# Attention and two MoE layers on one core: another hand-planned order of the steps up to the last block

## The chip, the cores and the metric

One core of a Trainium2 chip runs the whole program in one launch. The metric is the device time in microseconds. Three runs of the kernel before took 759.48, 760.04 and 760.96 us; the profile is of one further execution.

## What is computed

```
scores = (q @ k.T) / 8 + alibi, only 0 <= i - j < 128      # 4 batches, 8 heads, 576 rows, head size 64
x  = softmax(scores) @ v                                   # as [2304, 512]
x  = (relu(x @ w_in) ** 2) @ w_out                         # w_in 512 x 2048, w_out 2048 x 512
on = x @ w_skip > 0                                        # second MoE, 8 experts of 512 x 1024 x 512
e  = argmax(x @ w_gate); g = softmax(x @ w_gate)[e]
out = x;  out[on] += g * (relu(x @ w1[e]) @ w2[e])
```

## The kernel before

The 2304 rows are 18 tiles of 128; two tiles are a block, so there are nine blocks. Every fp32 factor of a large product is split into a high part and the rest (fp32r), and a product takes three matmuls: high x high, high x rest, rest x high.

The program up to the last block is a list of **steps**. A string of 1647 steps (line 879) is read from left to right by `piece` (line 1000), and each step issues its instructions under `manual_schedule` (line 1026), so the list sets the order in each of the five queues (TensorE, VectorE, ScalarE, Pool, SP). Between queues only the data's semaphores hold: an instruction starts when it is the first of its queue and its inputs and buffers are ready. A step's letter says what it is, the numbers which, and a last letter v, a or p puts it on VectorE, ScalarE or Pool where there is a choice:

- Attention of tile t: `l` loads q and k, or v (SP, L379, L382); `H` takes the high part of q and k (kh, L74), `L` the rest (kl, L392); `S` is the scores (TensorE, L408); `D` adds the bias and takes the row's extreme (VectorE from PSUM, L437); `E` the exponentials (ScalarE, L448); `M`, `N` guard and invert the sum (L458, L462); `O` normalises (L475 on ScalarE, L477 on VectorE, two instructions); `T` transposes (TensorE, L484), `U` copies that out (pts, L74); `V` multiplies by v (TensorE, L509); `Y` and `Z` write the two parts of the block's x (L74, L531).
- Weights of the first MoE, 32 chunks that come as 64-bit words: `w` loads (SP, L849), `j a b c d` turn them into floats in place (L94 or L96, then VectorE L100, L103, L108, L113), `e` and `f` write the two parts (L74, L125; `f` on Pool unless marked).
- First MoE of block n, pair fp of hidden chunks: `A` twelve products into ph (TensorE, L564), `r s g i` relu, square, high part gh, rest gl (L574, L580 or L582, L74, L592), `B` twelve products into acc (TensorE, L616).
- Routing of block n: `P Q` copy acc out, `p` (TensorE, L668), `q` copies lgs (ScalarE, L675), `m` (TensorE, L680), `o C F G J K k` choose experts and ranks, `W` writes the lists (Pool, L795); `t` transposes x2T (TensorE, L699), `x` copies it to xt (ScalarE, L706) and issues its two transfers, to x2d and to out (L709, L710). There is one xt buffer.

Behind the list stand the last block's first MoE, in which the first experts' weights are already loaded and split (from line 1048), and the second MoE expert by expert (from line 1129). Neither is touched.

All 32 weight chunks are converted while blocks 0 and 1 are multiplied, so for the first 133 us VectorE has both this and the softmax to do; after that TensorE's products set the pace.

Of the kernel before, what the change touches and what calls it, by code (L numbers as in the profile page):

```python
# [19 lines left out]
def attn_moe_kernel(  # L20
# [262 lines left out]
    with ExitStack() as mctx, ExitStack() as actx:  # L283
# [574 lines left out]
        def split(c):  # L858
# [27 lines left out]
            Z0 M1.2 w7 j7 w8 a7 U1.1 N1.2 H3.0 d5 b7 c4 w9 E2.1 c7 O1.2a N2.0 U1.0 d4 M2.1 j9 j6
            l1.1 V1.0 O1.3 a9 T1.3 N2.1 a6 O2.0a U1.3 T1.2 f1 U1.2 O2.1a b9 e4v w12 w10 L2.1
            S2.1 b6 H3.1 V1.1 e5v c6 c9 f0 d2 Y1a T2.0 U2.0 T2.1 j8 Z1 d9 A0.0.0 A0.0.1 w11 j11
            U2.1 D2.3 E2.3 a11 a8 D2.2 l2.1 V2.0 M2.3 e2 f3 b8 E2.2 N2.3 O2.3a d7 r0.0 M2.2 w13
            c8 j10 L3.0 S3.0 N2.2 O2.2a d6 d8 a10 T2.3 U2.3 s0.0a g0.0 e8v b10 D3.0 e9 b11 c10  # L890
            E3.0 f4 A0.1.0 T2.2 U2.2 D3.1 E3.1 j12v c11 a12 L3.1 j13 e7v M3.0 b12 M3.1 f2 N3.0
            f5 e6 c12 A0.1.1 a13 O3.0a f8 j16 A0.2.0 N3.1 d11 V2.1 i0.0p B0.0.0 S3.1 b13 r0.1
            O3.1a d10 T3.0 U3.0 D3.2 B0.0.1 Y2a E3.2 a16 T3.1 c13 s0.1a Z2 M3.2 U3.1 d13 g0.1v
            e13 e11 N3.2 O3.2a d12 i0.1 f9 A0.2.1 e12v r0.2 D3.3 E3.3 s0.2a f12v b16 M3.3 l3.1
            V3.0 f6 B0.1.0 w17 w15 T3.2 U3.2 j17v N3.3 A0.3.0 e10v a17 b17 c16 O3.3a g0.2 i0.2
            c17 f7 f13 A0.3.1 j14 a14 T3.3 b14 U3.3 f11 B0.2.1 j15 a15 b15 w18 c15 c14 r0.3 V3.1
            B0.1.1 Y3a Z3 d14 f10 B0.2.0 A1.0.0 A1.0.1 s0.3a d15 d17 g0.3 i0.3 e15 f15v j18 e14
            d16 f14v e17 A1.1.0 e16 A1.1.1 r1.0 s1.0a f16v a18 w19 B0.3.1 g1.0 i1.0 b18 j19 r1.1
            s1.1a c18 d18 e18 a19 b19 c19 d19 f17 B0.3.0 e19v f19v w20 g1.1 w21 j20v a20 j21 a21
            b20 b21 c20 c21 d20 e20 A1.2.0 f18 A1.2.1 A1.3.0 i1.1p d21 w22 w23 j22v A1.3.1  # L900
            B1.0.0 e21 B1.1.0 f20v a22 b22 B1.0.1 j23 r1.2 c22 f21v a23 B1.1.1 s1.2a g1.2 i1.2
            B1.2.1 r1.3 A1.4.0 s1.3a A1.4.1 b23 c23 A1.5.0 d22 g1.3v B1.2.0 l4.1 e22 d23 f22v
            w25 j25 e23v a25 b25 c25 d25 w24 j24 a24 i1.3 B1.3.1 e25v A1.5.1 B1.3.0 b24 c24 d24
# [344 lines left out]
```

## Time and profile before

| | |
|---|---|
| median of three runs | 760.04 us (759.48 to 760.96) |
| the profiled execution | 760.54 us, of which the instructions span 758.6 us |
| TensorE busy | 704.0 us, 93% of the span |
| VectorE, ScalarE, Pool busy | 447.4, 370.0, 178.9 us |
| granted TensorE clock, mean | 0.990 |
| the list of steps | ends at about 541 us; the rest takes 217.6 us |

The profile names an instruction by engine, line and tiles (`gl<-r,gh`: gl is written, r and gh are read) and gives its start and length in us. PE is TensorE, DVE VectorE, ACT ScalarE, POOL GpSimd. In brackets stands how long the engine had been idle before the instruction and what released it. An instruction that is blocked once it has been issued shows no idle time: it is only longer.

### The profile page before, as it was taken

How to read it: one execution, taken by the hardware profiler on the slowest of the kernel's cores; microseconds unless marked ns; L12 is line 12 of the kernel's file. 1: busy time of each engine (PE TensorE's matmuls, PEld its weight loads, DVE VectorE, ACT ScalarE, POOL GpSimd, SP SyncE). 2: the span in 40 equal slices, each digit the busy share in tenths (PEclk: the TensorE clock that was granted, in tenths of full speed). 3: DMA queues.
4: the chain of work that ended last, by engine and by line, in shares of the span. 5: the costliest groups of instructions: out<-in, count | busy, mean ns of one | idle time of the engine just before them, and what ended most of it. 6: DMA issues, size and time to landing. Idle time of an engine off the chain costs nothing. (4 is left out here: it accounts for less than half of the span.)

```text
span 758.6 us, 14480 instructions
## 1 busy us (share of the span) xinstructions
PE 704.0 (93%) x5620; PEld 639.6 (84%) x5620; DVE 447.4 (59%) x1140; ACT 370.0 (49%) x803; POOL 178.9 (24%) x166
## 2 busy tenths in 40 slices
PE   4588999998999999999999999999999789999994
PEld 3376999887999999999998999998999567777773
DVE  8999999664563544544354456332547627538871
ACT  6887555453453455343523434432346427437751
POOL 5364210222103402112022323211310511211220
PEclk9999999999999999999999999999999989999998
DMA  9513344014010130201010110024336377719840
GB/s 353 214 46 122 100 165 140 29 43 153 29 42 16 57 111 2 70 1 44 29 42 16 56 43 16 1 71 143 108 108 213 113 279 253 274 34 315 317 155 5
DMA packets 27682, 82.11 MB, mean 108 GB/s; under 512 B 4188, under 2 KB 4444, under 8 KB 27584
## 3 DMA queue, kind: packets, MB, share of 16 engines
...
HBM read 69.31 MB, written 12.49 MB: 108 GB/s over the span
## 5 line engine op out<-in xcount | busy, mean ns | idle before, releaser
L616 PE MATMUL acc<-gh,w2h_out 128*128 128x256 f32 x576 | 97.8, 292 | 0.9 <-ACT gh L74 0.8
L564 PE MATMUL ph<-xh,w1h_in 128*128 128x256 f32 x576 | 95.0, 287 | 0.6 <-DVE w1h_in L74 0.6
L616 PE MATMUL acc<-gl,w2h_out 128*128 128x256 f32 x576 | 92.8, 283 | 0.9 <-DVE gl L592 0.8
L564 PE MATMUL ph<-xh,w1l_in 128*128 128x256 f32 x576 | 92.5, 282 | 0.3 <-DVE w1l_in L125 0.3
L616 PE MATMUL acc<-gh,w2l_out 128*128 128x256 f32 x576 | 92.2, 282 | 0.0
L564 PE MATMUL ph<-xl,w1h_in 128*128 128x256 f32 x576 | 91.9, 282 | 0.0
L592 POOL TENSOR_TENSOR gl<-r,gh 128x512 fp32r<-128x512 f32 x33 | 44.1, 1336 | 189.4 <-ACT gh L74 110.0
L448 ACT ACTIVATE pr<-pr,stat 128x256 f32<-128x256 f32 (+1 forms) x144 | 70.1, 489 | 38.0 <-DVE stat L437 37.8
L574 ACT ACTIVATE r<-ph 128x512 f32<-128x512 f32 x72 | 42.7, 593 | 91.2 <-PE ph L564 57.8
L616 PEld LDWEIGHTS acc<-gh,w2h_out 128*128 128x128 f32 x576 | 78.6, 190 | 1.8 <-ACT gh L74 1.3
L616 PEld LDWEIGHTS acc<-gl,w2h_out 128*128 128x128 f32 x576 | 78.8, 189 | 1.5 <-DVE gl L592 1.5
L564 PEld LDWEIGHTS ph<-xh,w1l_in 128*128 128x128 f32 x576 | 78.6, 188 | 1.1 <-DVE w1l_in L125 0.5
L564 PEld LDWEIGHTS ph<-xh,w1h_in 128*128 128x128 f32 x576 | 78.4, 189 | 1.2 <-ACT sz L94 0.8
L616 PEld LDWEIGHTS acc<-gh,w2l_out 128*128 128x128 f32 x576 | 78.7, 189 | 0.0
L564 PEld LDWEIGHTS ph<-xl,w1h_in 128*128 128x128 f32 x576 | 78.5, 188 | 0.0
L484 PE MATMUL pt<-ident,pr 128*128 128x128 f32 x272 | 47.0, 296 | 8.0 <-ACT pts L74 5.6
L509 PE MATMUL pv<-pts,vt 128*64 128x128 f32 x544 | 40.1, 289 | 8.6 <-ACT pts L74 7.4
L158 DVE TENSOR_TENSOR w1l_e<-raw_e,w1h_e 128x1024 fp32r<-128x1024 f32 x31 | 36.7, 1224 | 16.2 <-ACT w1h_e L157 16.2
L475 ACT ACTIVATE pr<-pr,stat 128x256 f32<-128x256 f32 (+1 forms) x80 | 34.4, 482 | 23.6 <-DVE stat L462 23.3
L484 PEld LDWEIGHTS pt<-ident,pr 128*128 128x128 f32 x272 | 32.0, 148 | 16.0 <-ACT pts L74 6.9
L582 POOL TENSOR_TENSOR r<-r 128x512 f32<-128x512 f32 x17 | 18.0, 1056 | 114.2 <-ACT r L574 114.2
L509 PEld LDWEIGHTS pv<-pts,vt 128*64 128x64 f32 x544 | 30.0, 141 | 15.4 <-ACT pts L74 8.6
...
## 6 DMA issues: line engine op xcount, KB each, us to landing
...
big_w1l<-in_w_mlp_dram SPq DMA_DIRECT2D x4, 512.0 KB, 10.3
```

The lines of the kernel that those rows point to most:

```text
L158: eng.tensor_tensor(lo, val, hi.bitcast(F32), op=ALU.subtract)
L448: nc.scalar.activation(pr[:, j, cols], pr[:, j, cols], AF.Exp, bias=st[:, 0, h : h + 1], scale=-1.0, accum_out=st[:, 1, h : h + 1],)
L475: nc.scalar.activation(p, p, AF.Copy, scale=r[:, c])
L484: nc.tensor.transpose(pt[:, j, o : o + P], pr[:, j, o : o + P], ident)
L509: nc.tensor.matmul(to, a, b_, start=(kk == kts[0]), stop=(kk == t), skip_group_check=True,)
L564: nc.tensor.matmul(ph[:, j, :], a[:, kc, fs], b_[:, kc, :], start=(j == 0 and kc == 0 and a is wh and b_ is xh), stop=(kc == KC - 1 and a ...
L574: nc.scalar.activation(r, phs.pop((n, fp)).rearrange("p a b -> p (a b)"), AF.Relu)
L582: eng.tensor_tensor(r, r, r, op=ALU.mult)
L592: eng.tensor_tensor(gl.rearrange("p a b -> p (a b)"), r, gh.rearrange("p a b -> p (a b)").bitcast(F32), op=ALU.subtract,)
L616: nc.tensor.matmul(acc[dc // 2][:, dc % 2, :], a[:, f0 + j, dsl], b_[:, j, :], start=(fp == 0 and j == 0 and dc % 2 == 0 and b_ is gh and ...
```

## The change

The string of steps is another one: the same 1647 steps, in a different order, planned with a margin of time kept around every Pool instruction. Nothing else differs. Some steps change their engine: `L` 18 times on Pool for 21, `f` 19 for 17, `s` 19 for 17, `i` 32 for 33; `U` 20 times on VectorE for 30; `O` 34 on VectorE for 32.

```diff
@@ -877,113 +877,113 @@
         order = """
-            l0.0 H0.1 H0.0 L0.0v w0 j0 l1.0 S0.0 H1.0 a0 b0 D0.0 w1 E0.0 D0.1 c0 w2 l2.0 L1.0v
...
+            l0.0 H0.0 L0.0v S0.0 H0.1 w1 j1 a1 b1 D0.0 D0.1 l1.0 H1.0 E0.0 M0.0 L0.1 L1.0v w0
...
         """
```

What moves is seen in the queues. The first place is ScalarE at the routing of block 0 (`x0.1` is the second COPY of xt before, `q0` the COPY of lgs). Before:

```order
L706 COPY xt_1_2232<-xp_1_2215 128x512
L709 DMA x2d<-xt_1_2232 128x512
L710 DMA out_dram<-xt_1_2232 128x512
L574 ACTIVATE r_1_2250<-ph_1_2199 128x512
L706 COPY xt_1_2268<-xp_1_2258 128x512
L709 DMA x2d<-xt_1_2268 128x512
L710 DMA out_dram<-xt_1_2268 128x512
L675 COPY lgs_2297<-lgp_2253 128x256
L448 ACTIVATE pr_1_2187,stat_2181<-pr_1_2187,stat_2181 128x256 x2
```

and now:

```order
L706 COPY xt_1_2262<-xp_1_2256 128x512
L709 DMA x2d<-xt_1_2262 128x512
L710 DMA out_dram<-xt_1_2262 128x512
L475 ACTIVATE pr_0_2147<-pr_0_2147,stat_2146 128x256 x2
L574 ACTIVATE r_1_2296<-ph_1_2204 128x512
L675 COPY lgs_2320<-lgp_2251 128x256
L448 ACTIVATE pr_2_2317,stat_2146<-pr_2_2317,stat_2146 128x256 x2
```

Before, lgs stood right behind two copies of xt that follow each other with one relu between; now the earlier copy of xt is further ahead, and a normalisation and a relu stand between xt and lgs. The second place is ScalarE at the end of the list, the routing of block 6 (`x6.1`, `x5.0`, `q6`). Before:

```order
L706 COPY xt_1_6518<-xp_1_6449 128x512
L709 DMA x2d<-xt_1_6518 128x512
L710 DMA out_dram<-xt_1_6518 128x512
L574 ACTIVATE r_6_6535<-ph_6_6415 128x512
L580 ACTIVATE r_6_6535<-r_6_6535 128x512
L706 COPY xt_0_6556<-xp_0_6546 128x512
L709 DMA x2d<-xt_0_6556 128x512
L710 DMA out_dram<-xt_0_6556 128x512
L675 COPY lgs_6563<-lgp_6548 128x256
```

and now:

```order
L706 COPY xt_1_6459<-xp_1_6425 128x512
L709 DMA x2d<-xt_1_6459 128x512
L710 DMA out_dram<-xt_1_6459 128x512
L726 ACTIVATE ex_6467<-dl_6464 128x16
L74 CAST gh_5_6495<-r_5_6423 128x512
L574 ACTIVATE r_6_6552<-ph_6_6440 128x512
L74 CAST gh_6_6555<-r_6_6552 128x512
L675 COPY lgs_6575<-lgp_6547 128x256
L726 ACTIVATE ex_6609<-dl_6606 128x16
L574 ACTIVATE r_7_6611<-ph_7_6481 128x512
L706 COPY xt_0_6613<-xp_0_6523 128x512
L709 DMA x2d<-xt_0_6613 128x512
```

The copy of lgs moved ahead of `x5.0`, and two relus, two high parts and two exponentials stand between the two copies of xt. The third place is Pool from the chunks of the second half of the weights to the last one (`w1l_in` and `w2l_out` are steps `f`, gl is `i`). Before:

```order
L125 TENSOR_TENSOR w1l_in_1007<-raw_1_846,w1h_in_1006 128x4x128
L125 TENSOR_TENSOR w2l_out_1009<-raw_2_925,w2h_out_1008 128x512
L592 TENSOR_TENSOR gl_1_1091<-r_1_1063,gh_1_1090 128x512
L125 TENSOR_TENSOR w2l_out_1009<-raw_3_1150,w2h_out_1008 128x512
L125 TENSOR_TENSOR w1l_in_1007<-raw_1_1308,w1h_in_1006 128x4x128
L592 TENSOR_TENSOR gl_5_1397<-r_5_1393,gh_5_1396 128x512
```

and now:

```order
L592 TENSOR_TENSOR gl_3_943<-r_3_925,gh_3_942 128x512
L125 TENSOR_TENSOR w1l_in_988<-raw_0_412,w1h_in_987 128x4x128
L125 TENSOR_TENSOR w1l_in_988<-raw_1_375,w1h_in_987 128x4x128
L592 TENSOR_TENSOR gl_0_1074<-r_0_1041,gh_0_1073 128x512
L592 TENSOR_TENSOR gl_1_1093<-r_1_1089,gh_1_1092 128x512
L125 TENSOR_TENSOR w2l_out_990<-raw_2_1222,w2h_out_989 128x512
L125 TENSOR_TENSOR w2l_out_990<-raw_2_1381,w2h_out_989 128x512
L125 TENSOR_TENSOR w1l_in_988<-raw_0_1436,w1h_in_987 128x4x128
L592 TENSOR_TENSOR gl_6_1499<-r_6_1470,gh_6_1498 128x512
```

In this stretch Pool has nine instructions for six, three of them two rests gl (`i`) and one rest of a weight more; with `f10`, and now also `f11`, which stand between Z3 and the rows shown, it is 11 for 7.

## Rows read from the trace of the kernel before

**Rows 1.** Busy time by stretch: each engine, (xN) instructions, granted PE clock, DMA share, GB/s.

```profile
0.00:80.00 80.00, 55.22 (x440) 46.10 (x441) 73.50 (x198) 61.20 (x157) 38.02 (x47) 1.00 0.46 174
80.00:135.00 55.00, 52.97 (x439) 52.18 (x438) 53.46 (x92) 29.71 (x50) 11.36 (x7) 1.00 0.44 141
135.00:515.00 380.00, 376.88 (x3455) 356.14 (x3454) 187.35 (x642) 163.46 (x433) 80.53 (x68) 1.00 0.13 43
```

**Rows 2.** Waits of PE up to 80 us: us in all, times, longest; first and last of nine.

```profile
PE pv L509 <- ACT pts L74: 7.0, 2, 5.9
...
PE acc L616 <- DVE gl L592: 0.6, 1, 0.6
```

**Rows 3.** The same view from 80 to 541 us; first and last of seven.

```profile
PE lgp L680 <- ACT lgs L675: 4.0, 2, 2.2
...
PE acc L616 <- DVE gl L592: 0.3, 1, 0.3
```

**Rows 4.** Timeline of PE, 0 to 120 us: start, us, engine, line, operation.

```profile
84.75 0.64 PE L616 MATMUL acc<-gh,w2h_out 128*128 128x256 f32 x4
85.23 0.64 PE L616 MATMUL acc<-gh,w2l_out 128*128 128x256 f32 x4
```

**Rows 5.** Timeline of all engines, 25.3 to 34.2 us.

```profile
25.63 1.37 POOL L125 TENSOR_TENSOR w1l_in<-big_w1h,w1h_in 128x512 fp32r<-128x512 f32 x1 [8.74 <-issue]
...
27.23 0.42 DVE L437 CUSTOM_DVE_ANT_0 pr<-sc,bias 128x256 f32<-128x256 f32 x1
...
28.18 1.74 POOL L125 TENSOR_TENSOR w1l_in<-big_w1h,w1h_in 128x512 fp32r<-128x512 f32 x1
...
28.70 1.51 DVE L74 CAST w2h_out<-big_w1h 128x512 fp32r<-128x512 f32 x1
...
33.53 0.41 DVE L103 TENSOR_SCALAR sz<-sz 128x512 int32<-128x512 int32 x1
33.86 0.68 DVE L108 SCALAR_TENSOR_TENSOR big_w1l<-big_w1l,sz 128x512 int32<-128x512 int32 x1
```

**Rows 6.** The same view, 13.9 to 15.6 us.

```profile
14.01 1.53 DVE L103 TENSOR_SCALAR sz<-sz 128x512 int32<-128x512 int32 x1
```

**Rows 7.** The same view, 132.8 to 135 us.

```profile
132.71 0.69 DVE L125 TENSOR_TENSOR w2l_out<-raw,w2h_out 128x512 fp32r<-128x512 f32 x1
...
133.32 1.52 DVE L74 CAST kh<-raw 128x512 fp32r<-128x512 f32 x1
```

**Rows 8.** The same view, 76 to 82 us.

```profile
77.86 0.68 DVE L531 TENSOR_TENSOR xl<-pv,xh 128x512 fp32r<-128x512 f32 x1
```

**Rows 9.** The same view, 173 to 186.5 us.

```profile
176.66 0.41 DVE L74 CAST kh<-raw 128x512 fp32r<-128x512 f32 x1
...
177.23 0.59 ACT L706 COPY xt<-xp 128x512 f32<-128x512 f32 x1
...
183.96 0.58 ACT L706 COPY xt<-xp 128x512 f32<-128x512 f32 x1 [4.59 <-DMA out_dram<-xt]
...
185.86 0.61 PE L680 MATMUL lgp<-sel,lgs 128*128 128x9 f32 x4 [2.18 <-ACT lgs L675]
```

**Rows 10.** The same view, 508 to 545 us.

```profile
530.12 0.58 ACT L706 COPY xt<-xp 128x512 f32<-128x512 f32 x1 [4.15 <-DMA out_dram<-xt]
...
532.02 0.61 PE L680 MATMUL lgp<-sel,lgs 128*128 128x9 f32 x4 [1.83 <-ACT lgs L675]
```

**Rows 11.** Groups by line and form, 0 to 560 us: xcount, busy us, mean ns, idle.

```profile
L448 ACT ACTIVATE pr<-pr,stat 128x256 f32<-128x256 f32 x128 | 63.9, 501 | 37.0 <-DVE stat L437 37.0
...
L592 POOL TENSOR_TENSOR gl<-r,gh 128x512 fp32r<-128x512 f32 x33 | 44.1, 1336 | 189.4 <-ACT gh L74 110.0 <-DVE gh L74 53.6 <-PE sc L416 12.4
L574 ACT ACTIVATE r<-ph 128x512 f32<-128x512 f32 x68 | 40.3, 593 | 84.7 <-PE ph L564 51.3 <-DVE gl L592 14.6 <-POOL gl L592 14.0
...
L477 DVE TENSOR_SCALAR pr<-pr,stat 128x256 f32<-128x256 f32 x62 | 25.8, 458 | 0.7
...
L592 DVE TENSOR_TENSOR gl<-r,gh 128x512 fp32r<-128x512 f32 x35 | 24.1, 688 | 14.9 <-ACT gh L74 13.9 <-issue 0.7
```

More of the change, by code (lines that the diff above doesn't have):

```diff
@@ L886, in attn_moe_kernel @@
[L886 to L903, printed above, removed]
@@ L958, in attn_moe_kernel @@
-            i5.4 A5.6.0 D13.1 E13.1 M13.1 A5.5.1 S13.1 H14.1v L14.1 r5.5 N13.1 O13.1 V12.1 T13.0
-            Y12 Z12 U13.0 D13.2 E13.2 s5.5p g5.5 i5.5 B5.4.0 T13.1 l13.1 D13.3 B5.4.1 A5.6.1
-            M13.2 N13.2 O13.2 E13.3 M13.3 U13.1 B5.5.1 V13.0 r5.6 s5.6a T13.2 U13.2v A5.7.0
-            A5.7.1 N13.3 O13.3a T13.3 U13.3v S14.0 g5.6v D14.0 E14.0 D14.1 V13.1 i5.6p r5.7 Y13
-            t4.0.0 B5.6.0 Z13 B5.5.0 A6.0.0 A6.0.1 s5.7a H15.0v L15.0 E14.1 M14.1 t4.0.3 S14.1
-            p4 t4.0.1 M14.0 l16.0 N14.0 t4.0.2 g5.7v i5.7p x4.0 B5.6.1 r6.0 l14.1 s6.0p g6.0
@@ new lines, in attn_moe_kernel @@
+            B0.0.0 O3.1a s0.1a f3 g0.1 i0.1 w19 f9 A0.2.1 Y2a B0.0.1 T3.1 Z2 D3.3 j13 a13 E3.2
+            M3.2 b13 E3.3 U3.1 M3.3 N3.2 O3.2a w15 N3.3 c13 d13 b16 e13v f12 j17v a17 f6 B0.1.0
+            O3.3a l3.1 A0.3.0 e10v V3.0 T3.2 U3.2 c16 r0.2 s0.2a g0.2 j14 f7 B0.1.1 d11 i0.2
+            e11v a14 b14 b17 c17 T3.3 U3.3 c14 f13 A0.3.1 r0.3 s0.3a V3.1 Y3a Z3 j15 j18 g0.3
+            d14 e14 d17 a15 d16 b15 f10 f14v a18 c15 j19v d15 a19 e15v B0.2.0 f11 B0.2.1 f15v
+            b19 e17 c19 A1.0.0 b18 c18 i0.3p d18 d19 e18v f18v A1.0.1 e16 f16 A1.1.0 f17 r1.0
@@ new lines, in attn_moe_kernel @@
+            s1.0a w20 j20v e19v B0.3.0 A1.1.1 g1.0 i1.0p B0.3.1 r1.1 s1.1a g1.1 a20 B1.0.0
+            B1.0.1 A1.2.0 b20 c20 A1.2.1 f19v w21 j21 a21 b21 w23 c21 A1.3.0 A1.3.1 d20 i1.1p
+            B1.1.0 r1.2 s1.2a g1.2v d21 B1.1.1 e20 f20v i1.2 e21 f21v w22 j22 a22 j23 a23 b22
+            r1.3 b23 c23 s1.3a g1.3 A1.4.0 A1.4.1 w25 i1.3 j25 B1.2.1 r1.4 w24 c22 d22 a25 d23
+            B1.2.0 b25 e22 j24 a24 e23 b24 f23v A1.5.0 B1.3.0 c24 s1.4a g1.4 c25 d25 e25v A1.5.1
+            d24 i1.4 B1.4.0 B1.3.1 f25v w26 e24 f24v A1.6.0 A1.6.1 r1.5 f22 j26v a26 b26 c26
@@ new lines, in attn_moe_kernel @@
+            E6.0 D6.1 t1.1.0 t1.1.2 t1.1.3 A2.0.0 t1.1.1 x1.1 A2.0.1 r2.0 P0 l8.0 Q0 s2.0 g2.0v
+            A2.1.0 l7.0 J1 H7.0v A2.1.1 S6.1 E6.1 p0 t0.1.0 t0.1.3 t0.1.1 M6.0 t0.1.2 x0.1 i2.0
+            B2.0.0 B2.0.1 N6.0 O6.0a r2.1 T6.0 A2.2.0 D6.2 q0 A2.2.1 E6.2 M6.2 m0 s2.1p g2.1v
+            i2.1 B2.1.0 B2.1.1 A2.4.0 A2.4.1 r2.2 s2.2p A2.3.0 M6.1 N6.1 O6.1a g2.2v N6.2 i2.2p
+            B2.2.1 o0 B2.2.0 C0 F0 G0 l6.1 U6.0v T6.1 r2.4 K0 s2.4 g2.4 O6.2 U6.1 k0 i2.4 D6.3
+            E6.3 A2.3.1 B2.4.0 W1 L7.0 t0.0.0 t0.0.2 t0.0.3 t0.0.1 V6.0 S7.0 M6.3 N6.3 x0.0
@@ new lines, in attn_moe_kernel @@
+            O6.3a T6.2 H7.1v B2.4.1 U6.2 T6.3 U6.3 A2.5.0 L7.1 r2.3 A2.5.1 V6.1 D7.0 D7.1 E7.1
+            S7.1 M7.1 E7.0 M7.0 H8.0 N7.1 N7.0 O7.0 s2.3p O7.1a g2.3v i2.3 T7.0 r2.5 U7.0v
+            A2.7.0 T7.1 A2.7.1 D7.2 E7.2 s2.5a Y6 M7.2 g2.5v i2.5 L8.0v B2.3.1 N7.2 O7.2 Z6
+            B2.3.0 U7.1 D7.3 E7.3 M7.3 N7.3 r2.7 H8.1v s2.7a g2.7 i2.7p A2.6.0 B2.5.1 S8.0 l9.0
+            H9.0v l7.1 V7.0 O7.3a T7.3 U7.3 A2.6.1 r2.6 T7.2 B2.5.0 D8.0 L8.1v D8.1 E8.1 B2.7.0
+            s2.6 B2.7.1 g2.6 i2.6 E8.0 M8.0 N8.0 B2.6.0 O8.0a S8.1 U7.2v V7.1 Y7a T8.0 B2.6.1 P2
@@ new lines, in attn_moe_kernel @@
+            Z7 A3.0.0 U8.0 Q2 A3.0.1 p2 q2 t2.0.0 r3.0 t2.0.3 s3.0 t2.0.2 D8.2 t2.0.1 l10.0
+            A3.1.0 M8.1 g3.0 i3.0 m2 l11.0 A3.1.1 B3.0.0 x2.0 r3.1 s3.1p g3.1 N8.1 O8.1 A3.2.0
+            A3.2.1 T8.1 A3.4.0 i3.1p B3.0.1 B3.1.1 J0 A3.4.1 r3.2 s3.2p o2 C2 F2 G2 K2 D8.3 k2
+            U8.1 E8.2 A3.3.0 A3.3.1 l8.1 V8.0 M8.2 L9.0v S9.0 N8.2 O8.2 T8.2 B3.1.0 g3.2v i3.2
+            E8.3 M8.3 N8.3 O8.3a U8.2v T8.3 r3.3 U8.3v B3.2.0 s3.3a g3.3v i3.3 B3.3.1 t2.1.0
+            t2.1.1 D9.0 B3.2.1 r3.4 s3.4p g3.4v B3.3.0 E9.0 M9.0 H9.1v D9.1 E9.1 M9.1 V8.1 L9.1
@@ new lines, in attn_moe_kernel @@
+            N9.1 S9.1 i3.4p t2.1.2 H10.0 N9.0 O9.0 t2.1.3 x2.1 A3.5.0 A3.5.1 r3.5 T9.0 U9.0 W0
+            L10.0v D9.3 E9.3 A3.6.0 M9.3 Y8a N9.3 O9.3 Z8 A3.6.1 O9.1a T9.1 U9.1v H10.1 B3.4.1
+            D9.2 L10.1v E9.2 M9.2 l9.1 V9.0 S10.0 N9.2 O9.2a s3.5 T9.3 U9.3v g3.5v i3.5p B3.4.0
+            A3.7.0 B3.5.1 T9.2 D10.0 E10.0 D10.1 M10.0 N10.0 r3.6 s3.6p U9.2 A3.7.1 S10.1 g3.6v
+            V9.1 Y9 Z9 O10.0a T10.0 i3.6p E10.1 l12.0 U10.0 B3.5.0 A4.0.0 M10.1 N10.1 l10.1
+            O10.1 D10.3 E10.3 H11.0v M10.3 N10.3 r3.7 T10.1 B3.6.1 s3.7a g3.7v i3.7 D10.2 E10.2
@@ new lines, in attn_moe_kernel @@
+            L11.0 M10.2 B3.6.0 B3.7.1 U10.1v A4.0.1 r4.0 B3.7.0 s4.0a S11.0 g4.0 V10.0 O10.3a
+            T10.3 A4.1.0 A4.1.1 A4.3.0 i4.0p r4.1 s4.1 A4.3.1 P3 Q3 B4.0.0 g4.1 U10.3 B4.0.1
+            i4.1 r4.3 A4.2.0 s4.3a B4.1.1 N10.2 O10.2a T10.2 B4.1.0 U10.2 H11.1v V10.1 t3.1.0
+            l13.0 t3.1.2 L11.1v g4.3v t3.1.3 i4.3p D11.0 D11.1 E11.0 M11.0 H12.0v A4.2.1 B4.3.1
+            r4.2 s4.2 Y10a Z10 A4.4.0 S11.1 E11.1 M11.1 p3 N11.0 q3 g4.2v i4.2p N11.1 H12.1v
+            t3.1.1 x3.1 B4.2.1 O11.0a A4.4.1 J2 W2 L12.1 B4.2.0 T11.0 U11.0v B4.3.0 m3 o3 l11.1
@@ new lines, in attn_moe_kernel @@
+            O11.1 A4.5.0 A4.5.1 T11.1 r4.4 C3 F3 L12.0v G3 l14.0 s4.4 K3 k3 g4.4v i4.4p r4.5
+            s4.5p D11.2 A4.6.0 A4.6.1 E11.2 U11.1v g4.5v B4.4.0 i4.5p A4.7.0 A4.7.1 B4.4.1 D11.3
+            E11.3 M11.3 V11.0 N11.3 O11.3a S12.0 T11.3 r4.6 s4.6p M11.2 g4.6 i4.6p N11.2 B4.5.0
+            O11.2 U11.3 B4.5.1 T11.2 U11.2 B4.6.1 t3.0.0 t3.0.2 t3.0.3 D12.0 D12.1 E12.0 V11.1
+            S12.1 E12.1 M12.1 t3.0.1 B4.6.0 H13.0 x3.0 M12.0 N12.0 O12.0 T12.0 Y11 Z11 A5.0.0
+            r4.7 A5.0.1 s4.7a D12.2 g4.7 i4.7 r5.0 s5.0 g5.0v A5.2.0 U12.0 A5.2.1 B4.7.1 B4.7.0
@@ new lines, in attn_moe_kernel @@
+            P4 i5.0 r5.2 A5.1.0 N12.1 O12.1 s5.2a A5.1.1 T12.1 L13.0 Q4 g5.2 i5.2p D12.3 A5.3.0
+            A5.3.1 U12.1 H13.1v r5.1 B5.0.0 B5.0.1 s5.1p l12.1 E12.2 L13.1v V12.0 E12.3 M12.3
+            N12.3 M12.2 S13.0 N12.2 O12.3a T12.3 U12.3 g5.1v i5.1 B5.1.0 O12.2 T12.2 r5.3 U12.2
+            D13.0 E13.0 B5.2.1 s5.3p B5.1.1 M13.0 N13.0 D13.1 V12.1 E13.1 S13.1 O13.0a T13.0
+            D13.3 E13.3 M13.1 N13.1 U13.0v Y12a O13.1a A5.4.0 B5.2.0 M13.3 N13.3 A5.4.1 Z12
+            T13.1 g5.3 i5.3 O13.3a H14.1v L14.1v r5.4 s5.4a B5.3.0 g5.4 D13.2 A5.5.0 E13.2
@@ new lines, in attn_moe_kernel @@
+            B5.3.1 M13.2 H14.0v i5.4 A5.5.1 N13.2 l16.0 U13.1 L14.0 S14.0 l13.1 V13.0 r5.5 O13.2
+            T13.2 s5.5a g5.5 i5.5 B5.5.1 A5.6.0 B5.4.0 U13.2v B5.5.0 A5.6.1 T13.3 U13.3 r5.6
+            s5.6 B5.4.1 V13.1 D14.0 t4.0.0 g5.6 i5.6p Y13a D14.1 E14.1 M14.1 E14.0 M14.0 N14.0
+            t4.0.1 t4.0.2 t4.0.3 x4.0 A5.7.0 A5.7.1 r5.7 s5.7a g5.7v i5.7 B5.6.0 J3 W3 B5.6.1
+            B5.7.0 B5.7.1 P5 Z13 Q5 A6.0.0 p4 S14.1 q4 O14.0 T14.0 U14.0v m4 o4 A6.0.1 N14.1
+            r6.0 s6.0p A6.1.0 A6.1.1 g6.0v i6.0 A6.2.0 A6.2.1 D14.2 E14.2 r6.1 s6.1 A6.4.0 g6.1v
@@ new lines, in attn_moe_kernel @@
+            r6.5 O15.1 l17.0 l15.1 T15.1 U15.1v N15.3 s6.5p D15.2 E15.2 A6.7.0 V15.0 g6.5v S16.0
+            O15.3 T15.3 U15.3 i6.5 M15.2 D16.0 A6.6.0 N15.2 O15.2 H17.0v A6.6.1 J4 r6.6 s6.6a
+            g6.6 T15.2 B6.5.1 U15.2 i6.6p E16.0 L17.0v A6.7.1 r6.7 D16.1 E16.1 M16.0 N16.0
+            B6.5.0 S16.1 H17.1 V15.1 O16.0 T16.0 W4 s6.7p g6.7 B6.6.1 Y15a Z15 i6.7p B6.7.1
+            D16.3 U16.0 E16.3 M16.3 M16.1 N16.1 O16.1a A7.0.0 A7.0.1 B6.6.0 A7.1.0 r7.0 s7.0a
+            T16.1 l16.1 U16.1v B6.7.0 N16.3 A7.1.1 V16.0 g7.0v i7.0p D16.2 E16.2 M16.2 N16.2
@@ new lines, in attn_moe_kernel @@
+            S17.0 r7.1 s7.1 g7.1v i7.1p O16.2 O16.3a T16.3 U16.3 A7.3.0 P6 T16.2 D17.0 D17.1 Q6
+            A7.2.0 A7.2.1 E17.0 M17.0 N17.0 E17.1 M17.1 r7.2 U16.2 O17.0 B7.0.0 B7.0.1 B7.1.0
+            s7.2a L17.1 S17.1 V16.1 N17.1 T17.0 D17.2 g7.2 A7.3.1 i7.2 B7.1.1 U17.0v O17.1a
+            T17.1 E17.2 M17.2 N17.2 r7.3 l17.1 s7.3a O17.2 g7.3v Y16a Z16 i7.3p A7.4.0 A7.4.1
+            r7.4 U17.1v V17.0 T17.2 U17.2 B7.3.1 D17.3 B7.2.0 B7.2.1 E17.3 M17.3 A7.5.0 N17.3
+            O17.3 T17.3 B7.3.0 U17.3 V17.1 Y17a s7.4p Z17 g7.4v t6.0.0 t6.0.2 t6.0.3 i7.4 t6.0.1
@@ L987, in attn_moe_kernel @@
+            x6.0 A7.5.1 p5 q5 r7.5 t6.1.0 t6.1.1 B7.4.1 A7.6.0 t6.1.2 t6.1.3 m5 o5 x6.1 C5 F5
+            A7.6.1 A7.7.0 s7.5p g7.5 G5 i7.5 K5 B7.5.0 t5.0.0 t5.0.3 t5.0.1 k5 B7.4.0 p6 r7.6
+            s7.6 g7.6 J5 t5.0.2 i7.6 A7.7.1 q6 B7.6.1 m6 o6 B7.6.0 C6 F6 r7.7 x5.0 B7.5.1 G6 K6
+            J6 s7.7 g7.7 t5.1.0 W5 t5.1.1 t5.1.3 t5.1.2 i7.7 k6 W6 x5.1
         """
```

112 lines of the change are left out of this document (30 added, 82 removed).

## The prediction

> **What bounds the kernel now.** I read the busy time by stretch first [rows 1]. From 135 to 515 us TensorE is busy 376.88 of 380 us, so nothing can be won there but the few waits. Before 80 us it is busy 55.22 of 80, while VectorE is busy 73.50; from 80 to 135 us both are nearly full (52.97 and 53.46 of 55). Then TensorE's waits [rows 2]: up to 80 us 24.8 us in nine kinds, the greatest for pts, 7.0, the least 0.6; from 80 to 541 us [rows 3] only 6.9 us in seven kinds, of which 4.0 are two waits of the routing product m (L680) for lgs. Behind 541 us the program is the same in both kernels.
>
> TensorE's own work does not change: the table names the same steps, and one step A or B of twelve products takes 1.43 us when nothing waits (groups of four start 0.48 us apart, [rows 4]). So what counts is time in which TensorE waits, and, up to about 133 us, how far VectorE's queue has come, since it makes the weights.
>
> VectorE's queue holds a loss that its operations don't have by themselves. At 28.70 a cast takes 1.51 us and ends 0.3 us after the Pool instruction that began at 28.18 [rows 5]; a cast of the same form takes 0.41 us elsewhere [rows 9]. From the one at 14.01 [rows 6] to the one at 133.32 [rows 7] I count 23 such long VectorE instructions, together 20.5 us over what the same forms take alone, 0.89 us each. VectorE operations that read PSUM (L437, at 27.23) keep their 0.42 us beside Pool [rows 5]. The page "SBUF — State Buffer" of the Trainium skill, section "Who interferes with whom", says why: the two engines share one pair of ports under an exclusive lock, and whoever comes second blocks for the whole instruction. The durations here agree.
>
> **The change, part by part.** The margin itself is no instruction: every step and its arithmetic stay, only places in the queues and the engine of some steps move. I counted steps in both tables up to three marks.
>
> *Term 1, up to the parts of block 1 (Z3, now at 77.86).* Ahead of Z3 VectorE has 133 instructions for 137 (a D counted once): one a, b, c, e and f fewer, one O more. With 0.41 us for a, b and e, 0.68 for c [rows 5, 9], 0.69 for f (L592 has its form) and two times 0.46 for O [rows 11] that is 2.60 less 0.92, so 1.7 us less. ScalarE has 89 in both and Pool 19 in both. Z3 starts at 77.86 with no idle time of VectorE before it [rows 8]: it stands in the queue, so I take the whole 1.7 us. Bounds: nothing, if the ScalarE chain sets the place, and 2.3 us, the five instructions (a, b, c and two e) that leave the queue ahead of Z1.
>
> *Term 2, from Z3 to the last conversion f31.* VectorE has 92 instructions in both tables: two f, three i and one d fewer, a, b, c, e, H and s one more each: 5 x 0.69 + 0.68 less (4 x 0.41 + 0.68 + 0.69) is 1.1 us less. Pool has 11 for 7 (the third place shown above has most of them). If each of the four costs VectorE the 0.89 us that one long instruction costs now, that is 3.6 us more, net 2.5 us more. The table now sets one more product step (A0.5.1, 1.43 us) ahead of the last B of block 1, which covers as much. What is left, 1.1 us, is less than term 1 gave: **terms 1 and 2 together, 0.6 us gained.** Bounds for the cost of a Pool instruction to VectorE: nothing, since a margin may set only PSUM readers beside it, and 1.12 us, the longest excess seen (at 14.01, 1.53 for 0.41). I stay at 0.89, the mean of the very same thing, because nothing in the program makes Pool wait for a planned time.
>
> *Term 3, the two waits for lgs.* At 177.23 ScalarE copies xt, and its transfer to out is issued; the next xt uses the same buffer, so its copy waits 4.59 us until 183.96; lgs (q0) is queued behind it and TensorE waits 2.18 us at 185.86 [rows 9]. At the end the same: xt at 530.12 after 4.15 us, and TensorE waits 1.83 us at 532.02 [rows 10]. In the changed order two B, T6.0 and two A stand on TensorE between p0 and m0, 6.1 us of work, where only the two A stood, and q0 is no longer right behind that copy; at the end q6 stands ahead of xt (the first and second place shown above). Both waits go: 4.0 us. Bounds: nothing if the freed chain meets another wait at once, 4.0 at most.
>
> *Term 4, new tight places.* I went through the distances in TensorE's work between a producer and its consumer. Three are shorter than any that now passes without a wait. B5.5.1 comes 2.3 us after A5.5.1 (S14.0, V13.0 and T13.2 between), and its chain is relu 0.59, a square and a copy that I take as long, and gl 0.69 [rows 11], 2.5 us, with an estimated 0.1 us at each of four hand-overs 2.9: 0.6 us of wait. T4.0 comes 3.2 us after S4.0, and its chain has two of 0.42 (L437), two of 0.50 (L448), two short ones and two of 0.46 (L477) [rows 5, 11], 2.8 us and, with the short ones and five hand-overs, some 3.7: 0.5 us. T6.0 stands 2.85 us behind the transposes of xt, ahead of whose product ScalarE has the copy, two issues and O6.0, 0.58 + 0.9 + 0.9 us, and perhaps a wait for the buffer: 0.3 us. Together 1.4 us lost; bounds 0 and 3.
>
> Sum: -0.6 - 4.0 + 1.4 = -3.2 us. The profiled execution took 760.54 us, so it would take 757.3. The median shown is 0.5 us lower (760.04); against it I forecast **756.8 us**. Less than 0.2% (1.5 us) can't be told from no change.
>
> By the rule of that page of the Trainium skill ("SBUF — State Buffer", the same section), with every added Pool instruction blocking for its whole 1.34 us [rows 11], four would cost 5.4 us in place of 3.6, and the sum would be 1.4 instead of 3.2 us gained.
>
> **The rivals.**
> *Collisions fall.* If the new places put VectorE's PSUM readers beside Pool, half of the 23 long instructions may go. Ten fewer are 8.9 us less, and with 1.1 and 1.7 from the queue's length VectorE is at f31 some 11 us earlier. TensorE has 24.8 us of waits before 80 us to give. Then -11 - 4 + 1.4: about 747. For it: the loss is there in the rows. Against it: Pool starts as soon as its input is there (f1 started at 25.63 [rows 5], though its place in the table is 36 steps behind e3, the cast of 28.70), so a plan's distance is not kept on the chip. 0.15.
>
> *Slower: VectorE is blocked more often.* Thirty Pool instructions stand ahead of f31 for 26. If each blocks for 1.12 us, that is 33.6 for 20.5 us, 13.1 more less 2.8 of shorter queue and 1.4 that is covered, 8.9; with terms 3 and 4 (-2.6) 6.3 us slower, 766. It decides from the point at which the loss passes 20.5 + 2.8 + 1.4 + 2.6, some 27 us, that is 31 long instructions of 0.89, or 27 of 1.0: from there on it takes all that term 3 gives. With 30 of 1.0 to 1.1 the time is 763 to 766. For it: four more chances, and VectorE is 97% busy there [rows 1]. A late weight load would show in the same place: w20 now waits for f17, which is behind i0.3 on Pool, and j20 on VectorE needs it. 0.25.
>
> *No change.* Term 3's time is taken by other waits (the one xt buffer already holds ScalarE up for 4.59 and 4.15 us [rows 9, 10]), and terms 1 and 2 cancel: 759 to 761.5. 0.20.
>
> **How the numbers follow.** My forecast (753 to 758.5) has 0.40. Faster by over 0.2% is that and the first rival, 0.55; within 0.2% 0.20; slower 0.25. The range leaves out the best half of the first rival and the worst half of the slower one: 748 to 764. Its lower end takes in term 4 at nothing and a cost of Pool near its lower bound; its upper end 30 long instructions of 1.0 us.
>
> **What would show it.** TensorE's waits for lgs at L680: none, or under 0.5 us. Busy time up to 80 us: VectorE still above 70 us, TensorE's waits there within 3 us of 24.8. Long VectorE instructions up to f31: 24 to 28. First product of block 1 about 1.5 us earlier than now, last conversion (now 132.71) about 132 to 134, the routing product m6 (now 532.02) about 529. Short waits at B5.5.1 and T4.0. I am wrong if the first product of block 1 moves by more than 4 us, if the stretch from 135 us to the end of the table shows waits of over 4 us, or if the part behind the table changes by more than 1 us.

## The result, and the profile after

The changed kernel takes 764.97 us (median of 11 runs), the kernel before 760.46 us beside it: ratio 1.0062, 95% interval 1.0041 to 1.0083. It is **slower by 0.6%**, where 756.8 us, 0.4% faster, was forecast. The profiled execution took 765.04 us, its instructions span 763.4 us for 758.6, mean granted clock 0.979 for 0.990.

The busy time by stretch of the changed kernel, columns as in [rows 1]:

```profile
0.00:80.00 80.00, 55.48 (x437) 46.75 (x438) 74.59 (x193) 60.53 (x156) 37.94 (x48) 0.91 0.46 174
80.00:135.00 55.00, 50.81 (x404) 49.87 (x404) 53.81 (x86) 25.32 (x42) 15.62 (x11) 0.97 0.39 130
135.00:515.00 380.00, 378.06 (x3452) 357.61 (x3451) 182.68 (x642) 170.89 (x445) 79.52 (x67) 1.00 0.13 45
```

Up to 80 us little is lost in sum. The granted clock of 0.91 there comes from two stretches in which it went to its lower level (mean 0.57 from 28 to 36 and 0.57 from 55 to 63 us). In the kernel before the clock's record starts only at 39.7 us, so the 1.00 in [rows 1] says nothing of the time ahead of that: its transposes (L484) start 0.21 us apart up to there and 0.11 from 40 to 60 us. From 80 to 135 us TensorE loses 2.2 us of busy time and some clock, Pool has 11 instructions for 7; from 135 to 515 us it gains 1.2 us. Its waits from 80 to 541 us (us in all, times, longest) are now led by another one than in [rows 3]; lgs is gone from the list:

```profile
PE acc L616 <- DVE w2h_out L74: 4.3, 2, 3.1
PE ph L564 <- DVE xl L531: 0.9, 1, 0.9
```

The longer of the two, in TensorE's timeline of the changed kernel:

```profile
86.05 0.63 PE L564 MATMUL ph<-xh,w1l_in 128*128 128x256 f32 x4
89.82 1.15 PE L616 MATMUL acc<-gh,w2h_out 128*128 128x256 f32 x4 [3.13 <-DVE w2h_out L74]
90.77 1.05 PE L616 MATMUL acc<-gh,w2l_out 128*128 128x256 f32 x4
91.62 1.05 PE L616 MATMUL acc<-gl,w2h_out 128*128 128x256 f32 x4
92.47 1.03 PE L616 MATMUL acc<-gh,w2h_out 128*128 128x256 f32 x4
93.33 0.66 PE L616 MATMUL acc<-gh,w2l_out 128*128 128x256 f32 x4
```

Behind the wait four groups start some 0.88 us apart instead of the 0.48 of [rows 4]: the clock has gone to its lower level, 1.2 GHz. By stretch, the third of them behind the second wait:

```profile
86.00:90.00 4.00, 0.86 (x7) 0.66 (x7) 3.95 (x5) 1.23 (x2) 2.55 (x2) 0.99 0.73 220
90.00:94.00 4.00, 4.00 (x22) 4.00 (x23) 3.90 (x7) 1.22 (x2) 1.15 (x1) 0.58 0.11 42
...
141.00:146.00 5.00, 4.92 (x28) 4.91 (x28) 1.41 (x3) 1.77 (x4) 1.39 (x2) 0.66 0.25 96
```

A granted clock of 0.58 over 4 us in which TensorE is busy is 1.7 us lost; the stretch behind the second wait (1.2 us, at 139) loses another 5 x 0.34 = 1.7. The same thing stood in the kernel before, behind its first wait for lgs [rows 9], and the prediction did not count it:

```profile
186.00:190.00 4.00, 4.00 (x22) 4.00 (x23) 1.80 (x10) 1.01 (x6) 0.00 (x0) 0.57 0.22 82
```

Why w2h_out (step e15) is late, in VectorE's timeline of the changed kernel:

```profile
80.85 1.52 DVE L100 TENSOR_SCALAR sz<-sz 128x512 f32<-128x512 f32 x1
...
84.17 1.81 DVE L108 SCALAR_TENSOR_TENSOR big_w2l<-big_w2l,sz 128x512 int32<-128x512 int32 x1
86.02 1.41 DVE L96 TENSOR_SCALAR sz<-raw 128x512 int32<-128x512 int32 x1
87.35 1.75 DVE L113 SCALAR_TENSOR_TENSOR big_w2l<-big_w2l 128x512 int32<-128x512 int32 x1
...
89.35 0.41 DVE L74 CAST w2h_out<-big_w2l 128x512 fp32r<-128x512 f32 x1
```

and in Pool's:

```profile
80.42 1.67 POOL L592 TENSOR_TENSOR gl<-r,gh 128x512 fp32r<-128x512 f32 x1 [3.24 <-ACT gh L74]
83.81 3.33 POOL L125 TENSOR_TENSOR w1l_in<-raw,w1h_in 128x512 fp32r<-128x512 f32 x2 [1.72 <-issue]
87.11 1.44 POOL L592 TENSOR_TENSOR gl<-r,gh 128x512 fp32r<-128x512 f32 x1
```

Four VectorE instructions ahead of e15 (a15, c15, j19, d15) each meet one of Pool's (i0.3, f16, f17, i1.0) and last 4.3 us longer together than their forms do alone. Without that e15 would end at 85.5 (89.76 less 4.3), ahead of the 86.7 at which TensorE begins to wait for it. In the list f16 stands 13 VectorE steps behind c15, the instruction that it blocks. Its input was there at 83.7, Pool was free, so it ran. The same is seen once more at the end of the stretch, here on Pool and on VectorE:

```profile
133.45 2.79 POOL L392 TENSOR_TENSOR kl<-raw,kh 128x512 fp32r<-128x512 f32 x2 [2.40 <-ACT kh L74]
...
133.58 2.94 DVE L103 TENSOR_SCALAR sz<-sz 128x512 int32<-128x512 int32 x2
```

These two of Pool's are L4.1 and L4.0, which stand behind f30 in the list. They meet b31 and b30, which stand ahead of f31, and make the two 2.2 us longer than the 0.41 that the form takes alone.

Over the start as a whole, up to f31, there are 29 long VectorE instructions with 28.9 us of excess, for 22 with 19.4 in the kernel before (the last of the 23 in the prediction, the cast at 133.32, comes behind f31). The split f31 comes 6.4 us later than in [rows 7]. It is no longer the last one: the changed list sets d30 and f30 behind it, and f30 ends at 141.85, 8.4 us behind the end of the last conversion of the kernel before:

```profile
139.13 0.69 DVE L125 TENSOR_TENSOR w2l_out<-raw,w2h_out 128x512 fp32r<-128x512 f32 x1
...
141.16 0.69 DVE L125 TENSOR_TENSOR w2l_out<-raw,w2h_out 128x512 fp32r<-128x512 f32 x1
```

Up to the end of f31, all excess counted, VectorE has 3.0 us less work at the forms' own durations (1.4 of them are d30 and f30, only moved behind it), 9.8 us more excess and 1.2 us less idle time. Ahead of Z3, where Pool has 19 instructions in both lists, the long ones already have 3.4 us more excess.

At the end of the list the wait has moved. ScalarE's timeline, then TensorE's, of the changed kernel:

```profile
534.14 0.58 ACT L706 COPY xt<-xp 128x512 f32<-128x512 f32 x1
...
540.40 0.59 ACT L706 COPY xt<-xp 128x512 f32<-128x512 f32 x1 [3.38 <-DMA out_dram<-xt]
...
544.43 0.58 ACT L660 COPY x2T<-acc 128x512 f32<-128x512 f32 x1
```

```profile
545.07 0.63 PE L668 MATMUL lgp<-x2T,wg 128*32 128x256 f32 x4 [1.77 <-ACT x2T L660]
```

x5.0 now stands behind r7.7 and runs at 534.14 (530.12 in [rows 10]). So x5.1 waits until 540.40 for the one xt buffer, with everything of the last block that ScalarE has queued behind it, and p7 waits for P7.

**Where 4.8 us of span come from.** Up to 85 us +0.4 (products with the same work ahead of them, 84.75 and 85.11). From there to 146 us the waits are 5.9 us for 2.0 and 3.4 us are lost at the lower clock: +7.3. Then to the end of the list the waits are 0.3 for 4.9, and the low clock behind lgs (1.7) is gone: -6.3. At p7 +2.6 (1.8 us of wait, 0.2 for the second half of x2T, and what follows it). That is 4.0; TensorE is in fact 4.2 us late behind p7, and 0.6 more comes in the part behind.

### The profile page after: what moved, and what is told of

It is laid out like the page before. It is cut to its first block, busy times and chain, and to the rows that moved or that the text cites. A ratio compares the mean times of both kernels' runs of the same rounds, so it can differ in the third digit from the quotient of the medians.

```text
span 763.4 us, 14483 instructions
## 1 busy us (share of the span) xinstructions
PE 707.1 (93%) x5620; PEld 642.3 (84%) x5620; DVE 446.4 (58%) x1135; ACT 372.7 (49%) x808; POOL 177.5 (23%) x166
## 5 line engine op out<-in xcount | busy, mean ns | idle before, releaser
L564 PE MATMUL ph<-xh,w1h_in 128*128 128x256 f32 x576 | 96.6, 290 | 0.3 <-DVE w1h_in L74 0.3
L448 ACT ACTIVATE pr<-pr,stat 128x256 f32<-128x256 f32 (+1 forms) x144 | 70.1, 490 | 40.3 <-DVE stat L437 40.3
L74 ACT COPY pts<-pt 128x512 f32<-128x512 f32 (+1 forms) x52 | 28.9, 557 | 47.4 <-PE pt L484 44.8
L484 PE MATMUL pt<-ident,pr 128*128 128x128 f32 x272 | 45.6, 289 | 4.4 <-ACT pr L475 2.9
L582 POOL TENSOR_TENSOR r<-r 128x512 f32<-128x512 f32 x19 | 20.4, 1075 | 116.0 <-ACT r L574 116.0
L437 DVE CUSTOM_DVE_ANT_0 pr<-sc,bias 128x256 f32<-128x256 f32 (+1 forms) x80 | 28.2, 391 | 26.1 <-PE pt L484 25.3
```

Source lines behind the costliest of these rows:

```text
L74: (nc.scalar.copy if eng is nc.scalar else eng.tensor_copy)(to, x)
L437: nc.vector.tensor_tensor_reduce(both(pr[:, j, cols]), both(scs[hp // 2][j][:, hp % 2, cols]), bias8[:, h, near, :], scale=-SCALE, scalar= ...
L448: nc.scalar.activation(pr[:, j, cols], pr[:, j, cols], AF.Exp, bias=st[:, 0, h : h + 1], scale=-1.0, accum_out=st[:, 1, h : h + 1],)
L484: nc.tensor.transpose(pt[:, j, o : o + P], pr[:, j, o : o + P], ident)
L564: nc.tensor.matmul(ph[:, j, :], a[:, kc, fs], b_[:, kc, :], start=(j == 0 and kc == 0 and a is wh and b_ is xh), stop=(kc == KC - 1 and a ...
L582: eng.tensor_tensor(r, r, r, op=ALU.mult)
```

## The experiments

Theory S: the loss sits in the start, where blocked VectorE instructions make w2h_out late, and at x5.1. Rival E: only the end of the list counts. Rivals N, R and others are named in the expectations. Ratios are to the kernel before, run beside each (its medians 761.5 to 762.6 us).

**1. Old start, new rest; new start, old rest.** Each list is cut behind f31 and goes on with the steps still missing, in the other's order.

```diff
-(changed list)
+(list before, up to f31) (changed list, without the steps already done)
```

> The kernel before up to its step f31 (last conversion of the first block's weights), then the changed table for the steps that are left. Theory S (the loss sits in the start: on VectorE more long instructions beside Pool, so w2h_out comes late, PE waits and its granted clock falls twice): the 7.5 us that PE lost from 85 to 145 us in the changed kernel go; what is left of the change is the gain at the first wait for lgs (2.2 us of wait and 1.7 us of low clock), the second wait gone (2.0) and the new wait for x2T behind the table (2.6): about 757 us, 755.5 to 758.5, so 0.3 to 0.7% faster than the kernel before. Rival E (the loss sits behind the table, where the copy x5.1 holds up ScalarE): still slower than before, 762 to 765. Last f31 at 132 to 134, first wait for lgs under 0.5.

> The changed kernel up to its step f31, then the old table for the steps that are left. Theory S: all of the start's loss and none of the gains: 760.5 + 7 = 767.5, 766 to 769.5; f31 near 139, PE waits for w2h_out of 4 us or more between 80 and 145 and stretches at a granted clock of 0.50 behind them; the wait of 1.8 us for lgs near 530 back. Rival E: as the kernel before, 760 to 762.

Measured: old start 0.9923 (0.9895 to 0.9950), 756.33 us, f31 ends at 133.3; new start 1.0111 (1.0080 to 1.0141), 770.24 us, f31 at 138.7. TensorE's longest waits from 80 to 560 us, first the old start's, then the new start's:

```profile
PE lgp L668 <- ACT x2T L660: 1.6, 1, 1.6
```

```profile
PE acc L616 <- DVE w2h_out L74: 6.8, 2, 3.6
PE lgp L680 <- ACT lgs L675: 4.1, 2, 2.5
```

So the change is two changes of opposite sign: a start that loses and a rest that gains. The first was the larger. Rival E falls. The new start took more than the expected 766 to 769.5: its second wait for w2h_out is 3.6 us long, where the changed kernel's is 1.2.

**2. x5.0 earlier.** One step of the changed list moved.

```diff
-q6 B7.6.1 m6 o6 B7.6.0 C6 F6 r7.7 x5.0
+q6 x5.0 B7.6.1 m6 o6 B7.6.0 C6 F6 r7.7
```

> The changed kernel with one step moved: x5.0 (a copy on ScalarE into xt and its two transfers out) straight behind q6 instead of behind r7.7, so that x5.1 finds xt free sooner. Theory S with the term behind the table: the wait for x2T near 543 (1.8 us, 2.6 us with what follows it) goes: 762.4, 761.5 to 763.3. Rival (that wait only takes up time that another wait would take): same as the changed kernel, 764 to 766.

Measured 0.9999 (0.9976 to 1.0022), 761.58 us: no longer slower than the kernel before. By the two ratios that is 0.6% of gain where 0.3% was expected. ScalarE's timeline there: the second copy no longer waits.

```profile
528.95 0.59 ACT L706 COPY xt<-xp 128x512 f32<-128x512 f32 x1
...
536.19 0.58 ACT L706 COPY xt<-xp 128x512 f32<-128x512 f32 x1
...
541.06 0.59 ACT L660 COPY x2T<-acc 128x512 f32<-128x512 f32 x1 [0.63 <-PE acc L616]
```

The wait for x2T is gone, and set against the changed kernel TensorE gains 2.7 us around p7, as priced: in this kernel the term is shown. In the two profiled executions another 1.4 us lie at 142 us, where the second low clock stayed away, at 1.00, though the wait ahead of it is the same. Whether that makes up the rest of the ratio in the other runs, which have no profile, stays open.

**3. x5.0 late in the kernel before.**

```diff
-t5.0.2 x5.0 J5 q6
+t5.0.2 J5 q6
 ...
-r7.7 G6
+r7.7 x5.0 G6
```

> The kernel before with one step moved: x5.0 behind r7.7, where the changed table has it. Theory S: the wait for lgs near 532 (1.8 us) goes, the wait for x2T behind the table (1.8 us, 2.6 with what follows it) comes instead: 760 to 762, no change that the runs can tell. Rival (x5.0 has nothing to do with the wait behind the table): 758 to 759, no wait for x2T.

Measured 0.9999 (0.9976 to 1.0022), 760.91 us. The wait for lgs near 532 went, but the one for x2T did **not** come. ScalarE's timeline:

```profile
531.46 0.57 ACT L706 COPY xt<-xp 128x512 f32<-128x512 f32 x1
...
537.10 0.59 ACT L706 COPY xt<-xp 128x512 f32<-128x512 f32 x1 [3.54 <-DMA out_dram<-xt]
...
540.75 0.59 ACT L660 COPY x2T<-acc 128x512 f32<-128x512 f32 x1
```

The place behind r7.7 alone does not do it, so the rival has this point. In the old rest ScalarE reaches r7.7 at 530.98, so x5.1 is done at 537.7 and P7 in time; in the changed one it is 533.66, 2.7 us later, while the last B of the list's blocks starts only 1 us later (537.94, 538.99). In these runs the wait of 1.8 us comes only where both are there, x5.0 behind r7.7 and a late r7.7; no run moves r7.7 by itself.

**4. The logits first, in the kernel before.**

```diff
-x0.1 A2.2.0 A2.2.1 q0 m0
+q0 x0.1 A2.2.0 A2.2.1 m0
 ...
-x5.0 J5 q6
+q6 x5.0 J5
```

> The kernel before with two steps moved on ScalarE: q0 ahead of x0.1 and q6 ahead of x5.0, so that the copy of the logits does not stand behind a copy that waits for xt's transfer out. Theory S prices these two waits, at 185.86 and 532.02, with what hangs on them: 2.2 us, 1.7 us for the 3.4 us at a granted clock near 0.50 behind the first, and 1.8 us: 760.5 - 5.7 = 754.8, 753.5 to 757. Rival (the wait only moves to the next reader, as x5.1 did in the changed kernel): 759 to 761, with a new wait for x2T or xp.

Measured 0.9954 (0.9934 to 0.9974), 758.01 us, 0.46% for an expected 0.75%, between the two ranges. Both waits for lgs went, and with the first its low clock. The second came back at the next reader, TensorE's transposes (waits from 145 to 560 us):

```profile
PE xp L699 <- ACT xt L706: 1.9, 1, 1.9
```

The first wait is thus worth having by itself, the second only together with the transfer that holds xt.

**5. More Pool steps, in the kernel before.** Eight subtractions put on Pool, as in the changed list. (That list takes others off Pool; here 34 Pool steps stand ahead of f31, 30 in the changed list, 26 before.)

```diff
-f12v f16v f22v f26v f28v i0.3 i1.0 i1.6
+f12 f16 f22 f26 f28 i0.3p i1.0p i1.6p
```

> The kernel before with eight subtractions (f12, f16, f22, f26, f28, i0.3, i1.0, i1.6) put from VectorE on Pool at the same places, which is where the changed table has them. Theory S (nearly every Pool subtraction blocks one VectorE instruction for about 0.95 us, a VectorE subtraction takes 0.69): 8 long instructions more, 7.6 us, against 5.5 us of work less: f31 ends 1 to 3 us later than in the kernel before (133.4), time 760 to 764. Rival R (Pool relieves VectorE): f31 near 128 to 130, time 757 to 760.

Measured 1.0104 (1.0083 to 1.0125), 769.52 us; f31 ends at 142.6, 9.2 us later. Rival R falls: VectorE has 5.5 us less work and is later. The size is more than S gave: 8.9 us more excess and 4.9 us more idle time (3.5 of it one wait whose releaser the profile doesn't name), and TensorE now waits for Pool's queue. The longest wait from 80 to 145 us:

```profile
PE acc L616 <- POOL gl L592: 4.5, 1, 4.5
```

**6. Two of the four blockers on VectorE, in the changed kernel.**

```diff
-e16 f16 A1.1.0 f17
+e16 f16v A1.1.0 f17v
```

> The changed kernel with two of its Pool steps, f16 and f17, on VectorE at the same places, which are 15 steps behind the conversion c15 that they blocked. Theory P (it counts which VectorE instruction is blocked: c15, j19 and d15 stand ahead of the conversion e15 that PE waits for at 86.5; Pool ran f16 and f17 early, since nothing ties them to VectorE): e15 comes 2 to 3 us earlier, PE's wait for w2h_out falls from 3.1 to under 1.2, the low clock behind it goes, and the time falls by 2 to 4 us: 761 to 763. Rival N (only the number counts: two long instructions less, 2.1 us, for 1.4 us of work more): the wait stays at 2.2 or more, 764 to 765.

Measured 1.0054 (1.0035 to 1.0074), 765.29 us. TensorE's timeline, at the old place and later:

```profile
87.82 0.73 PE L616 MATMUL acc<-gh,w2h_out 128*128 128x256 f32 x4 [1.01 <-DVE w2h_out L74]
...
117.23 1.22 PE L616 MATMUL acc<-gl,w2h_out 128*128 128x256 f32 x4 [3.15 <-DVE gl L592]
118.25 1.05 PE L616 MATMUL acc<-gh,w2h_out 128*128 128x256 f32 x4
```

Theory P was right on the wait (3.1 to 1.0, and the clock holds behind it) and wrong on the time: VectorE is still late, f31 ends 1.9 us later than in the changed kernel, and the same lateness is met at 117 with a low clock of its own. So VectorE's whole queue has to be on time, not one conversion.

**7. Both gains together.** The old start, the changed rest, and x5.0 behind q6.

```diff
+(e1_old_start) with q6 x5.0 B7.6.1 ... r7.7 B7.5.1
```

> The old start with the changed rest (as in e1_old_start) and x5.0 straight behind q6 (as in e3_x5_early). Theory S, two separate terms that add: 756.3 less 3 to 4 for the wait for x2T near 535: 752.8, 751.5 to 754.5, 1% faster than the kernel before. Rival (the terms share a cover): 755.5 to 757.

Measured **0.9904 (0.9885 to 0.9922)**, 754.76 us: 1.0% faster, as expected, in time just above the range. The wait at p7 is gone, but against experiment 1 that is 0.2% (1.6 us of the medians) for the 3 to 4 us expected, and the two intervals overlap, so the runs don't show that the second term adds in full. TensorE's waits from 80 to 541 us, the first and the last of five; together 2.3 us, where [rows 3] had 6.9:

```profile
PE acc L616 <- ACT gh L74: 0.8, 1, 0.8
...
PE acc L616 <- DVE gl L592: 0.3, 1, 0.3
```

**8. Pool steps on VectorE.** First all 30 of the changed start, then, on the kernel of 7, the four weight subtractions behind Z3 at their places in the list, then the same four where Pool had in fact run them.

```diff
+(e4)  every f, L and i on Pool up to f31 on VectorE
+(e10) f17v f18v f23v f25v
+(e12) f16v f17v ... b19 f18v ... e23v f23v ... e25v f25v
```

> The changed kernel with every subtraction that Pool does up to f31 (19 f, 6 L and 5 i steps) put on VectorE at the same place. Theory S (a Pool subtraction costs VectorE about as much as, or more than, doing it itself): the long VectorE instructions of the start, 31.6 us over nominal in the changed kernel, fall under 5 us; VectorE takes 30 instructions of about 0.69, so 20.7 us, more; f31 comes at 139.1 - 26.6 + 20.7 = 133, 130 to 135, the waits for w2h_out fall under 2 us, and the time is 757 to 760. Rival (VectorE has no room, Pool's help is worth its blocking): f31 behind 142, time over 768.

> The kernel of e7_old_start_x5 with the four Pool subtractions of weights behind Z3 (f17, f18, f23, f25) on VectorE at the same places, where what they read is long done, so that VectorE waits for nothing there (in e4_no_pool it waited). Theory S: four blocked instructions less, 3.9 us in the kernel before (0.84, 1.01, 1.00, 1.01), against 2.8 us of work more: f31 ends at 132.0 to 133.0 instead of 133.45, time 753 to 755. Rival R (Pool's help is worth its blocking): f31 at 135 to 136.5, 756 to 758.

> As e10_four_on_vector, with the four VectorE subtractions moved forward to where Pool had in fact run them (f17 behind f16, f18 behind b19, f23 behind e23, f25 behind e25). Theory B (what went wrong there was the raw tile: Pool had set it free early by running ahead of VectorE's queue, and the next weight load waited for it): the waits of ScalarE for weight loads, 18.5 us there from 90 to 135 us, fall under 3, f31 ends at 132 to 134 instead of 143.8, time within 0.4% of e7_old_start_x5, 752 to 757. Rival R (VectorE simply has no room for these four): f31 at 136 or later, 758 or more.

Measured: e4 1.0365 (1.0333 to 1.0396), 790.13 us, f31 at 160.7; e10 1.0031 (1.0006 to 1.0056), 763.94 us, f31 at 143.8; e12 **0.9871 (0.9844 to 0.9897), 753.54 us**, f31 at 133.2. In e4 the time is where the rival put it, over 768. The excess of the start went, as S had it, but VectorE now stands idle, 31 us up to 139.8 (6.8 in the changed kernel), so it is not full, as the rival supposed; its longest wait up to 140 us is for ScalarE:

```profile
DVE gl L592 <- ACT gh L74: 6.8, 2, 6.4
```

e4 so tells nothing of the price of a blocked instruction. e10 is slower than both ranges and showed a reason that neither theory had. ScalarE's waits from 90 to 135 us in e10, then in the kernel of 7, then in e12:

```profile
ACT sz L94 <- DMA raw<-in_w_mlp_dram: 18.5, 4, 6.2
```

```profile
ACT sz L94 <- DMA raw<-in_w_mlp_dram: 0.9, 1, 0.9
```

```profile
ACT sz L94 <- DMA raw<-in_w_mlp_dram: 4.4, 3, 2.9
```

Weights are loaded into few raw tiles, and the subtraction f is a tile's last reader. On Pool it runs as soon as its cast is done, well ahead of its place; on VectorE it waits its turn, and the next load with it. Put where Pool had run them, the four cost nothing: VectorE has four f more (some 2.7 us) up to f31, four blocked instructions fewer (17 for 21), and the same f31. (The wait for loads did not fall under the 3 us expected, but to 4.4.)

e12 and the kernel of 7 both beat the kernel before and the changed one; their intervals overlap, so the runs can't tell between the two.

## Why the prediction was wrong

**The step that failed is term 2**, with term 1 in front of it: "If each of the four costs VectorE the 0.89 us that one long instruction costs now, that is 3.6 us more". I put a price on the four added Pool instructions and left the loss of the old ones as it was; in term 1, with 19 of Pool's in both lists, I priced none. The runs show the whole pattern new: 29 long instructions up to f31, where 22 had been, and 1.00 us each instead of 0.89. That is 9.5 us for 3.6, of which 3.4 lie ahead of Z3. The shorter queue of VectorE was real up to f31 (3.0 us by the forms' own times, 2.8 forecast), but Z3 came 1.2 us later instead of 1.7 earlier, f31 at 139.1 instead of 132 to 134. And 1.4 of the 2.8 us were no gain: I took f31 for the last conversion in both lists, while in the changed one d30 and f30 stand behind it. And I had the reason in hand, under the first rival: Pool starts as soon as its input is there, so a plan's distance is not kept. I used it against fewer collisions and not for more.

In the rows above c15 starts 0.4 us behind f16 on Pool and ends 0.5 us behind f16's end (85.43), where it takes 0.68 us alone: it hardly got on until f16 was done. The Trainium skill's page "SBUF — State Buffer", section "Who interferes with whom", says that of a VectorE instruction that needs the shared ports: the second to issue blocks until the first is done. The trace agrees.

**What the delay costs TensorE was missing altogether.** I had VectorE's 1.1 us covered by a product step. 6.4 us are not covered, and each long wait brought some 1.7 us at the lower clock.

**Term 3 was right in its mechanism.** The first wait for lgs went, and it was worth 3.9 us (2.2 and the low clock of 1.7), not 2.2. The second went too, and came back behind the list as 1.8 us, 2.6 with what follows. That is the bound "nothing if the freed chain meets another wait at once", which I had named and not looked for: x5.0 was itself moved, and what ScalarE has queued behind x5.1 lies in code that the list doesn't touch. "Behind 541 us the program is the same" was true of the code and not of its time.

**Term 4 was too large**: none of its three places waits; from 146 us to the end of the list there is one wait of 0.3 us, at a scores product at 159.35, for 1.4 forecast.

**The rival that came true** is the slower one, VectorE blocked more often, with 0.25. Its threshold, "27 of 1.0", was passed by 29 of 1.0, and 763 to 766 holds the 765 measured, though partly by chance: it knew neither the low clock nor x5.1. Its late load for j20 was not it: none of VectorE's waits up to 140 us is for a load. Of the signs, the long instructions (24 to 28), f31, the part behind the list (over 1 us) spoke against the forecast; busy time up to 80 us (74.6), TensorE's waits there (24.3 us) and the lgs waits held; the first product of block 1 came 0.8 us earlier (78.28) for 1.5; m6 came at 532.30, not at 529.

What stays open: the blocking could not be taken away by itself with all steps in place, so its share in the start's loss rests on the accounting (3.0 less, 9.8 more, 6.4 late) and on experiments 5 and 6, not on one run alone.
